# Another split of the tokens over the partitions, and counts and search one slot later, in attention followed by mixture of depths

## The chip, the cores and the metric

One core of a Trainium2 chip runs the whole kernel. The metric is the device time of one execution in microseconds; the time before is the median of three runs, 308.45 us (307.94 to 308.86).

## What is computed

Two steps, joined by a change of layout. With B = 8 batches, 8 heads, 576 tokens, head width 64, in float32:

```
q_s = softmax(q, over the 64 of a head)       k_s = softmax(k, over the 576 tokens)
attn = q_s @ (k_s.T @ v)                      per batch and head
x    = attn with its heads side by side       (8, 576, 512)

scores = x @ w_gate                           (8, 576)
top    = the 128 tokens of each batch with the highest score
out    = x
out[top] = x[top] + sigmoid(scores[top]) * (relu(x[top] @ w1) @ w2)
```

w1 is 512 x 1024, w2 is 1024 x 512. The input q, k and v are 9.4 MB each.

## The kernel before, in words

The work is cut into 16 units: unit u is batch u // 2 and four of its heads (`units`, L76). For a unit the 576 tokens lie five to a partition on partitions 0 to 63 (tokens 0 to 319) and four to a partition on partitions 64 to 127 (tokens 320 to 575), so a tile of q, k or v is 128 x 4 heads x 5 tokens x 64, and the fifth place of the upper half stays zero. `load(u, which)` (L84) brings each tensor with two DMAs on SyncE's queue (SP), one for each half: 64 partitions, 4 heads, pieces of 1,280 or 1,024 bytes. Three buffers each for q, k and v (`LD`) let loads run ahead; `load(u)` waits until the exponentials and the copy of unit u - 3 have read the buffer.

`prepare(u)` (L458) takes the exponentials of q and k on ScalarE and copies v next to a column of ones on VectorE. `kv_mm` (L178) multiplies k's exponentials with v, `kv_out` (L190) makes the block-diagonal right operand from it (with a last column for the gate's scores), `q_t` and `q_t_last` (L206, L218) transpose q's exponentials on TensorE, `x_mm` (L227) multiplies, and `x_out` (L239) normalizes on VectorE and, with a unit's second half done, stores x with two DMAs on SP. `score(b)` adds up a batch's gate scores.

The choice of the 128 tokens of batch b: `score_row(b)` (L267) spreads all scores over a row on every partition (transposes on TensorE, copies on ScalarE); `compare(b)` (L281) compares on VectorE each token's score with the row, tokens of equal score by their order; `count(b)` (L296) adds these up with matmuls against ones, which gives each token its rank; `pick(b)` (L314) searches, on VectorE, for the token of each rank (lines L322), makes its index, and POOL issues a gather of the 128 rows from the stored x (L327). Then `turn(b)` (L337) transposes the gathered rows on TensorE, `mlp1` and `mlp2` (L348, L363) are eight pieces each, 4 x 2 matmuls of 128 columns or 1 x 2 of 512, and `finish(b)` (L370) adds the result and scatters it from POOL.

The order on every engine is written out by hand (L473 to L551). Slot s does unit s, and kv_mm and q_t of unit s + 1, prepares unit s + 2 and loads unit s + 5; from slot 4 on, eight pieces of the MLP are spread over each slot, mlp1 of batch (s - 4) // 2 in even slots, mlp2 in odd ones. An odd slot ends with score_row; in the even slot that follows stand compare, later count and pick, and the even slot after that begins with turn. The parts of w1 and w2 are loaded on SP behind the loads of slots 0 to 4 (L528), so the first mlp1 pieces need the fourth part of w1, issued in slot 2. Each engine works in program order, and so does each DMA queue.

PSUM has three groups of banks, "tp" and "mm" with two banks each, "x" with two of double size. Before the first loads have come, 30 small matmuls keep TensorE busy (`WARM`, L107). A second path (`general`, with `shift`) runs only where sums leave a range, which they don't here; it changes with the layout and costs nothing.

Of the kernel before, what the change touches and what calls it, by code (L numbers as in the profile page):

```python
# [17 lines left out]
def kernel(  # L18
# [23 lines left out]
    P = 128  # L42
    R = 5
    N2 = R - 1
    S2 = 64 * R
# [7 lines left out]
    WARM = 30  # L53
    assert S == 64 * (R + N2) and D == 64 and DM == H * D and DM == 512 and H % 4 == 0
    assert 1 < capacity < S and KF == 8 and NQ == 2
    HALF = S // 2
# [39 lines left out]
    load(0, "qkv")  # L96
    load(1, "qkv")
    load(2, "qkv")
# [26 lines left out]
    nc.vector.memset(side, 0.0)  # L125
    v_ones, kv_diag = [], []
    for n in range(2):
        t = const.tile([P, 4, R, D + 1], F32, name=f"v_ones{n}")
        nc.vector.memset(t[:, :, :, D:], 1.0)
        nc.vector.memset(t[part(1), :, N2, D:], 0.0)  # L130
# [13 lines left out]
    tok_row = const.tile([P, S], F32, name="tok_row")  # L144
    rows4 = tok_row[:, :N2 * P].rearrange("p (r h c) -> p r h c", r=N2, h=2)
    nc.gpsimd.iota(rows4[:, :, 0], pattern=[[1, N2], [R, 64]], base=0, channel_multiplier=0,
                   allow_small_or_imprecise_dtypes=True)
    nc.gpsimd.iota(rows4[:, :, 1], pattern=[[1, N2], [N2, 64]], base=S2, channel_multiplier=0,
                   allow_small_or_imprecise_dtypes=True)
    nc.gpsimd.iota(tok_row[:, N2 * P:], pattern=[[R, 64]], base=N2, channel_multiplier=0,  # L150
                   allow_small_or_imprecise_dtypes=True)
# [87 lines left out]
    def x_out(u, i):  # L239
# [20 lines left out]
    chunks = [(slice(0, P), slice(r * P, (r + 1) * P)) for r in range(N2)] + [(slice(0, 64), slice(N2 * P, S))]  # L260

    def score(b):
        s = md.tile([P, R], F32, tag="s", name="s")
        nc.vector.reduce_sum(out=s, in_=sr.pop(b).rearrange("p a i r h -> p r (a i) h"), axis=AX.XY)
        st["s", b] = s

    def score_row(b):  # L267
        s = st["s", b]
        srow = md.tile([P, S], F32, tag="srow", name="srow")
        t_ps = bank("tp", 2)  # L270
        for r in range(N2):
            nc.tensor.transpose(out=t_ps[:, r * P:(r + 1) * P], in_=s[:, r:r + 1].to_broadcast([P, P]),
                                identity=ident)
        nc.scalar.copy(out=srow[:, :N2 * P], in_=t_ps)
        l_ps = bank("tp", 2)
        nc.tensor.transpose(out=l_ps[:, :64], in_=s[:64, N2:].to_broadcast([64, P]),
                            identity=ident[:64, :64])
        nc.scalar.copy(out=srow[:, N2 * P:], in_=l_ps[:, :64])
        st["srow", b] = srow

    def compare(b):  # L281
        s, srow = st["s", b], st["srow", b]
        less = md.tile([P, R, S], BF16, tag="less", name="less", bufs=1)
        ties = md.tile([P, R, P], BF16, tag="ties", name="ties", bufs=1)
        for j, (rows, cols) in enumerate(chunks):
            own = s[rows, j:j + 1]
            nc.vector.tensor_scalar(less[rows, j, :cols.stop], srow[rows, :cols.stop], own, None, op0=OP.is_lt)  # L287
            if cols.stop < S:
                nc.vector.tensor_scalar(less[rows, j, cols.stop:], srow[rows, cols.stop:], own, None,  # L289
                                        op0=OP.is_le)  # L290
            width = cols.stop - cols.start
            nc.vector.scalar_tensor_tensor(ties[rows, j, :width], srow[rows, cols], own, after[rows, :width],  # L292
                                           op0=OP.is_equal, op1=OP.mult)
        st["cmp", b] = less, ties

    def count(b):  # L296
        less, ties = st.pop(("cmp", b))
        rank = md.tile([P, S], F32, tag="rank", name="rank")
        for e in range(2):
# [3 lines left out]
            for j, (rows, cols) in enumerate(chunks):  # L303
                todo.append((rows, less[rows, j, lo:hi], 0, HALF))
                a, z = max(lo, cols.start), min(hi, cols.stop)
                if a < z:
                    todo.append((rows, ties[rows, j, a - cols.start:z - cols.start], a - lo, z - lo))
            for n, (rows, rhs, a, z) in enumerate(todo):
                nc.tensor.matmul(out=r_ps[:, a:z], lhsT=ones_b[rows, :P], rhs=rhs, start=(n == 0),  # L309
# [4 lines left out]
    def pick(b):  # L314
# [3 lines left out]
        for n, (k0, m) in enumerate(slots):  # L318
            sel = sl.tile([P, 2], F32, tag="sel", name="sel")
            for c, row in enumerate((tok_row, srow)):  # L320
                junk = md.tile([P, S], BF16, tag="junk_p", name="junk_p")
# [63 lines left out]
    def shift(u):  # L385
# [4 lines left out]
        nc.vector.tensor_max(m[part(0)], m[part(0)], kr[part(0), :, N2])  # L390
# [12 lines left out]
        for h in range(4):  # L403
            for n, rows in enumerate((R, N2)):
                o = kr[part(n), h, :rows]
                nc.vector.tensor_sub(o, o, row[part(n), h][:, None].to_broadcast([64, rows, D]))
# [5 lines left out]
    def general():  # L412
        for b in range(B):
            for u in (NQ * b, NQ * b + 1):
                load(u, "qkv")
# [42 lines left out]
    def prepare(u):  # L458
        q_exp(u)
        k_exp(u)  # L460
        v_copy(u)

# [10 lines left out]
    with tc.manual_schedule():  # L473
        prepare(0)
        load(3, "qkv")
# [8 lines left out]
        load(4, "qkv")  # L484

        number = None
        for s in range(NU + LAG):
# [14 lines left out]
            chosen = (s - 2) // 2 if s % 2 == 0 and 2 <= s <= NU else None  # L502
# [23 lines left out]
            if s + 5 < NU:  # L526
                load(s + 5, "qkv")
# [4 lines left out]
            if chosen is not None:  # L532
                compare(chosen)
# [5 lines left out]
            pieces(2)  # L539
            if ends is not None:  # L540
                score_row(ends)
# [3 lines left out]
            pieces(3)  # L545
            if last:
                pieces(1)
            if busy and odd == 1:
# [31 lines left out]
```

## Time and profile before

| | us |
|---|---|
| median of three runs | 308.45 (307.94 to 308.86) |
| the profiled execution's own time | 308.41 |
| its span in the profile | 306.6 |
| TensorE busy (matmuls) | 252.0, 82% |
| VectorE busy | 135.3, 44% |
| ScalarE busy | 98.7, 32% |
| POOL busy | 19.2, 6% |
| mean granted TensorE clock | 0.905 |

The span runs from the first instruction to the last; 1.8 us of the time lie outside it. A busy share is a mean over the whole span, and busy matmuls are not matmuls at full speed: the granted clock has two levels, 1.2 GHz (shown as 0.50) and 2.4 GHz (1.00). The chain of waits follows the end of the span backwards, from each instruction to what released it. The timeline lists an engine's instructions in order, equal ones merged (xN), with the idle time before them in brackets. Windows give each engine's busy time in a stretch, the granted clock, the share in which the 16 DMA engines were busy, and the bytes per second that they moved.

### The profile page before, as it was taken

The page shows a single profiled execution, that of the slowest core. Times are in us where ns is not written, and L with a number is a line of the kernel's source. Part 1 is how long each engine was busy: PE and PEld are TensorE (multiplying, and loading weights), DVE is VectorE, ACT ScalarE, POOL GpSimd, SP SyncE. Part 2 cuts the span into 40 slices and gives each one's busy share as a digit, 9 for nine tenths or more (in the row PEclk, how much of TensorE's full clock was granted, in tenths as well). Part 3 has the DMA queues.
Part 4 walks back from the last instruction along what each step waited for, and adds up shares of the span by engine and source line. Part 5 has one row for each costly group of instructions (what it writes and reads, how often), then busy time and mean ns, then how long its engine had stood idle before and what let it go on. Part 6 is the DMA issues. An engine that isn't in the chain of part 4 may idle for free.

```text
span 306.6 us, 5131 instructions
## 1 busy us (share of the span) xinstructions
PE 252.0 (82%) x1991; PEld 196.8 (64%) x1991; DVE 135.3 (44%) x494; ACT 98.7 (32%) x178; POOL 19.2 (6%) x33
## 2 busy tenths in 40 slices
PE   4267784825689998999989998999799989998991
PEld 4246682714677686867867685769585967583850
DVE  2125647711174538252754376336624484351000
ACT  2355542511042533252516251526134311120100
POOL 4000000100001010101010100010010101101101
PEclk9999977765599999699979997999689998999997
DMA  6999999999999596909792779331213031301000
GB/s 148 230 231 232 241 272 234 284 291 235 290 253 270 166 249 165 236 2 219 167 252 51 199 172 239 78 79 44 69 34 80 34 79 34 77 36 36 34 6 37
DMA packets 39328, 46.67 MB, mean 152 GB/s; under 512 B 2945, under 2 KB 36737, under 8 KB 39297
## 3 DMA queue, kind: packets, MB, share of 16 engines
q1 hardware_dynamic: 37472, 41.95, 57.9%
q0 software_dynamic: 1280, 4.20, 4.1%
q8 instruction: 17, 0.28, 0.4%
q10 hardware_dynamic: 544, 0.13, 0.2%
q14 instruction: 15, 0.11, 0.1%
HBM read 34.73 MB, written 11.53 MB: 151 GB/s over the span
## 4 chain that ended last, share of the span: by engine, by line
PE 67%; DVE 16%; DMA 9%; issue 2%; ACT 2%; SPq 1%; POOL 0%; POOLq 0%; DVEq 0%; ACTq 0%
PE mm L367 19%; PE mm L357 16%; PE x L233 12%; PE tp L186 8%; PE tp L213 6%; PE tp L309 4%; DVE less L287 4%; DMA out_dram<-xs 4%; DMA w<-in_moe_w_dram 3%; DVE ties L292 3%; DMA v<-in_v_dram 3%; DVE less L289 2%; DVE xs L249 2%; DVE v_ones L176 2%; SPq L91 1%
## 5 line engine op out<-in xcount | busy, mean ns | idle before, releaser
L357 PE MATMUL mm<-xT,w 128*128 128x128 f32 x512 | 73.5, 303 | 7.7 <-DMA w<-in_moe_w_dram 6.3
L357 PEld LDWEIGHTS mm<-xT,w 128*128 128x128 f32 x512 | 68.9, 216 | 10.5 <-DMA w<-in_moe_w_dram 6.6
L367 PE MATMUL mm<-w,hT 128*128 128x512 f32 x128 | 60.9, 602 | 0.0
L233 PE MATMUL x<-kv_diag,qT 128*128 128x132 f32 x320 | 43.7, 287 | 0.0
L233 PEld LDWEIGHTS x<-kv_diag,qT 128*128 128x128 f32 x320 | 41.7, 202 | 2.4 <-issue 2.4
L186 PE MATMUL tp<-v_ones,ke 128*64 128x65 f32 x640 | 26.8, 250 | 14.0 <-DVE after L158 8.8
L186 PEld LDWEIGHTS tp<-v_ones,ke 128*64 128x64 f32 x640 | 24.4, 162 | 17.1 <-issue 10.5
L367 PEld LDWEIGHTS mm<-w,hT 128*128 128x128 f32 x128 | 22.0, 190 | 17.5 <-issue 16.7
L215 ACT ACTIVATE qT<-tp,krec 128x512 f32<-128x512 f32 x32 | 22.0, 687 | 32.4 <-PE tp L213 32.3
L249 DVE TENSOR_TENSOR xs<-x,qrec 128x384 f32<-128x384 f32 x64 | 31.4, 491 | 2.2
L309 PE MATMUL tp<-less,ones_b 128*128 128x288 bf16 (+1 forms) x80 | 21.8, 329 | 12.2 <-DVE less L287 5.3
L309 PEld LDWEIGHTS <-ones_b 128*128 128x128 bf16 (+1 forms) x128 | 11.5, 104 | 27.0 <-issue 20.5
L248 DVE RECIPROCAL qrec<-x 128x6 f32<-128x6 f32 x64 | 11.8, 184 | 36.6 <-PE x L233 36.2
L375 DVE SCALAR_TENSOR_TENSOR o<-mm,g,xr 128x512 f32<-128x512 f32 x8 | 6.0, 751 | 44.3 <-PE mm L367 44.3
L172 ACT ACTIVATE qe<-q 128x640 f32<-128x640 f32 x32 | 21.6, 726 | 4.5 <-DMA q<-in_q_dram 4.5
L213 PE MATMUL tp<-ident,qe 128*128 128x128 f32 x128 | 22.7, 307 | 0.2 <-DVE prod L200 0.2
L165 ACT ACTIVATE ke<-k 128x1280 f32<-128x1280 f32 x16 | 20.1, 1258 | 1.2 <-DMA k<-in_k_dram 1.2
L360 ACT ACTIVATE hT<-mm 128x512 f32<-128x512 f32 x16 | 9.6, 598 | 31.5 <-PE mm L357 31.5
L213 PEld LDWEIGHTS tp<-ident,qe 128*128 128x128 f32 x128 | 17.2, 159 | 3.8 <-issue 2.6
L195 DVE RECIPROCAL krec<-tp 128x2 f32<-128x2 f32 x16 | 2.7, 170 | 38.0 <-PE tp L186 38.0
L327 POOL DMA_INDIRECT xr<-out_dram,idx x8 | 7.9, 987 | 177.2 <-DVE g L333 77.7
L311 ACT COPY rank<-tp 128x288 f32<-128x288 f32 x16 | 6.4, 399 | 36.2 <-PE tp L309 36.2
(65 smaller groups left out, 190.6 us busy)
## 6 DMA issues: line engine op xcount, KB each, us to landing
q<-in_q_dram SPq DMA_DIRECT2D x16, 320.0 KB, 10.1
k<-in_k_dram SPq DMA_DIRECT2D x16, 320.0 KB, 6.4
v<-in_v_dram SPq DMA_DIRECT2D x16, 320.0 KB, 6.8
out_dram<-xs SPq DMA_DIRECT2D x16, 320.0 KB, 4.0
q<-in_q_dram SPq DMA_DIRECT2D x16, 256.0 KB, 9.9
k<-in_k_dram SPq DMA_DIRECT2D x16, 256.0 KB, 6.3
v<-in_v_dram SPq DMA_DIRECT2D x16, 256.0 KB, 7.3
out_dram<-xs SPq DMA_DIRECT2D x16, 256.0 KB, 4.0
```

The lines of the kernel that those rows point to most:

```text
L165: nc.scalar.activation(out=ke, in_=raw["k"][u % LD], func=AF.Exp)
L172: nc.scalar.activation(out=qe[:, i], in_=qr[:, i], func=AF.Exp)
L186: nc.tensor.matmul(out=kv[part(h), i], lhsT=ke[:, 2 * i + h, r], rhs=vo[:, 2 * i + h, r], start=(r == 0), stop=(r == N2))
L213: nc.tensor.transpose(out=t_ps[:, r * P:(r + 1) * P], in_=qe[:, i, r].rearrange("p h d -> p (h d)"), identity=ident)
L215: nc.scalar.activation(out=st["qT", u][:, i, :N2].rearrange("p r c -> p (r c)"), in_=t_ps, func=AF.Copy, scale=krec[:, u, i:i + 1])
L233: nc.tensor.matmul(out=x[:, r // 3, r % 3], lhsT=qT[:, i, r], rhs=kv_diag[u % 2][:, i], start=True, stop=True)
L248: nc.vector.reciprocal(out=rec[:, rows], in_=o[:, :, :, D])
L249: nc.vector.tensor_mul(xs[b][:, rows, qd, i], o[:, :, :, :D], rec[:, rows].to_broadcast([P, rows.stop - rows.start, 2, D]))
L287: nc.vector.tensor_scalar(less[rows, j, :cols.stop], srow[rows, :cols.stop], own, None, op0=OP.is_lt)
L309: nc.tensor.matmul(out=r_ps[:, a:z], lhsT=ones_b[rows, :P], rhs=rhs, start=(n == 0), stop=(n == len(todo) - 1), skip_group_check=True)
L357: nc.tensor.matmul(out=h_ps[:, f % 4 * m:(f % 4 + 1) * m], lhsT=w1[:, d, f * P:(f + 1) * P], rhs=xT[:, d, :m], start=(d == 0), stop=(d == ...
L367: nc.tensor.matmul(out=st["y", b, n][:m], lhsT=st["hT", b, n][:, f, :m], rhs=w2[:, f], start=(f == 0), stop=(f == KF - 1))
```

## The change

The new tile has nine tokens in each pair of partitions: an even partition takes five, the odd one after it the next four. So each of the two DMAs of a tensor reaches every second partition of all 128, and so does each store. A row of scores has 640 places for 576, of which 64 are no tokens: `valid` is 1 on even and 0 on odd partitions, `beyond` is 0 and the lowest number, and the fifth score is valid * s + beyond. So the choice is made over five full chunks of 128 instead of four and a half.

The fifth places are zeroed over all partitions before the loads, on VectorE for the first buffers and on POOL for the others. Loads, and the exponentials of prepare, come in the order k, v, q. The warm-up is 20 float32 matmuls of 132 columns and 20 small ones.

In the order by hand, compare stays in the even slot; count and pick move to the odd slot behind it, after q_t_last and one more piece; score_row moves behind three more pieces. In the last slot of the units (15), score_row and compare of the last batch follow directly on the count of the batch before; slot 16 counts and picks the last batch. `turn` stays at the head of its even slot.

```
@@ def load @@
-            for n, (rows, s0) in enumerate(((R, 0), (N2, S2))):
+            for n, rows in enumerate((R, N2)):
                 nc.sync.dma_start(
-                    out=t[part(n), :, :rows].rearrange("p h r d -> p h (r d)"),
-                    in_=bass.AP(tensor=src.tensor, offset=first + s0 * D,
-                                ap=[[rows * D, 64], [SD, 4], [1, rows * D]]))
-
-    load(0, "qkv")
-    load(1, "qkv")
-    load(2, "qkv")
+                    out=t[n::2, :, :rows].rearrange("p h r d -> p h (r d)"),
+                    in_=bass.AP(tensor=src.tensor, offset=first + n * R * D,
+                                ap=[[9 * D, 64], [SD, 4], [1, rows * D]]))
+
+    for n in range(LD):
+        for what in "kvq":
+            (nc.vector if n == 0 else nc.gpsimd).memset(raw[what][n][:, :, N2], 0.0)
+    load(0, "kvq")
+    load(1, "kvq")
+    load(2, "kvq")
...
+    ones_f = const.tile([P, P + 4], F32, name="ones_f")
+    nc.vector.memset(ones_f, 1.0)
     w_ps = bank("tp", 2)
+    for n in range(20):
+        nc.tensor.matmul(out=w_ps[part(n % 2), :132], lhsT=ones_f[:, :64], rhs=ones_f, start=True, stop=True)
     for n in range(WARM):
         nc.tensor.matmul(out=w_ps[:, :P], lhsT=ones_b[:, :P], rhs=ones_b[:, :P], start=True, stop=True)
-    for n in range(LD):
-        for what, engine in (("q", nc.gpsimd), ("k", nc.vector), ("v", nc.gpsimd)):
-            engine.memset(raw[what][n][part(1), :, N2], 0.0)
...
@@ def x_out @@
-            for n, (rows, s0) in enumerate(((R, 0), (N2, S2))):
+            for n, rows in enumerate((R, N2)):
                 nc.sync.dma_start(
-                    out=bass.AP(tensor=out.tensor, offset=out[b, s0].offset + 4 * D * qd,
-                                ap=[[rows * DM, 64], [DM, rows], [1, 4 * D]]),
-                    in_=xs[b][part(n), :rows, qd].rearrange("p r i h d -> p r (i h d)"))
+                    out=bass.AP(tensor=out.tensor, offset=out[b, n * R].offset + 4 * D * qd,
+                                ap=[[9 * DM, 64], [DM, rows], [1, 4 * D]]),
+                    in_=xs[b][n::2, :rows, qd].rearrange("p r i h d -> p r (i h d)"))
@@ def score @@
+        nc.vector.scalar_tensor_tensor(s[:, N2:], s[:, N2:], valid, beyond, op0=OP.mult, op1=OP.add)
@@ def score_row @@
+        srow = md.tile([P, RP], F32, tag="srow", name="srow")
+        for r0, r1 in ((0, N2), (N2, R)):
+            t_ps = bank("tp", 2)
+            for r in range(r0, r1):
+                nc.tensor.transpose(out=t_ps[:, (r - r0) * P:(r - r0 + 1) * P],
+                                    in_=s[:, r:r + 1].to_broadcast([P, P]), identity=ident)
+            nc.scalar.copy(out=srow[:, r0 * P:r1 * P], in_=t_ps[:, :(r1 - r0) * P])
@@ def compare @@
+        less = md.tile([P, R, RP], BF16, tag="less", name="less", bufs=1)
+        for r in range(R):
+            own, end = s[:, r:r + 1], (r + 1) * P
+            nc.vector.tensor_scalar(less[:, r, :end], srow[:, :end], own, None, op0=OP.is_lt)
+            if end < RP:
+                nc.vector.tensor_scalar(less[:, r, end:], srow[:, end:], own, None, op0=OP.is_le)
+            nc.vector.scalar_tensor_tensor(ties[:, r], srow[:, r * P:end], own, after,
                                            op0=OP.is_equal, op1=OP.mult)
...
@@ def prepare @@
-        q_exp(u)
         k_exp(u)
         v_copy(u)
+        q_exp(u)
@@ slots @@
-            chosen = (s - 2) // 2 if s % 2 == 0 and 2 <= s <= NU else None
+            compared = (s - 2) // 2 if s % 2 == 0 and 2 <= s < NU else None
+            chosen = (s - 3) // 2 if s % 2 == 1 and 3 <= s < NU else None
+            if s == NU:
+                chosen = B - 1
...
-            if chosen is not None:
-                compare(chosen)
+            if compared is not None:
+                compare(compared)
             pieces(1)
             if s + 1 < NU:
                 q_t_last(s + 1)
             else:
                 pieces(1)
-            pieces(2)
-            if ends is not None:
-                score_row(ends)
+            pieces(1)
             if chosen is not None:
                 count(chosen)
                 pick(chosen)
-            pieces(3)
+            if last:
+                score_row(ends)
+                compare(ends)
+            pieces(2)
             if last:
                 pieces(1)
+            pieces(1)
+            if ends is not None and not last:
+                score_row(ends)
+            pieces(1)
             if busy and odd == 1:
                 each(finish, mlp_b)
```

count and pick work over 640 columns for 576, two halves of 320 for 288, with the same operations.

## Rows read from the trace of the kernel before

**Rows 1.** The chain of waits in order of time (start us, us, what)

```profile
12.66 0.83 DVE v_ones L176
...
69.70 9.85 DMA w<-in_moe_w_dram
...
79.60 0.79 PE mm L357 x2
...
250.07 1.00 PE tp L309 x8
...
271.37 1.82 PE tp L309 x16
```

**Rows 2.** The page, part 2: mean busy share of the DMA engines, 40 slices

```profile
DMA  6999999999999596909792779331213031301000
```

**Rows 3.** Windows of 3 us, first and last: clock, DMA share, GB/s

```profile
3.00:6.00 3.00, 1.85 (x18) 1.58 (x15) 0.45 (x4) 0.01 (x1) 0.95 (x5) 1.00 1.05 231
...
30.00:33.00 3.00, 2.16 (x48) 2.12 (x49) 1.19 (x3) 0.91 (x3) 0.00 (x0) 1.00 1.12 236
```

**Rows 4.** Windows of 1 us, the same columns

```profile
44.00:45.00 1.00, 1.00 (x11) 1.00 (x10) 0.93 (x5) 0.58 (x1) 0.00 (x0) 1.00 1.10 363
...
100.00:101.00 1.00, 1.00 (x11) 1.00 (x10) 0.20 (x1) 0.41 (x1) 0.00 (x0) 1.00 1.05 387
...
157.00:158.00 1.00, 1.00 (x7) 1.00 (x6) 1.00 (x3) 0.00 (x0) 0.00 (x0) 0.50 1.00 256
...
162.00:163.00 1.00, 1.00 (x6) 0.44 (x3) 0.17 (x1) 0.53 (x2) 0.00 (x0) 1.00 0.36 102
```

**Rows 5.** The page, part 6: DMA issues, with size and us to landing

```profile
out_dram<-xs SPq DMA_DIRECT2D x16, 256.0 KB, 4.0
```

**Rows 6.** Timeline of TensorE, slots 1, 8, 9: start us, us, instruction, [idle before]

```profile
30.84 1.39 PE L186 MATMUL tp<-v_ones,ke 128*64 128x65 f32 x40 [2.18 <-DVE v_ones L176]
...
149.77 1.95 PE L357 MATMUL mm<-xT,w 128*128 128x128 f32 x16
...
151.68 0.30 PE L309 MATMUL tp<-less,ones_b 128*128 128x288 bf16 x1
...
156.43 4.37 PE L357 MATMUL mm<-xT,w 128*128 128x128 f32 x24
...
160.72 1.39 PE L186 MATMUL tp<-v_ones,ke 128*64 128x65 f32 x40
...
163.44 1.29 PE L233 MATMUL x<-kv_diag,qT 128*128 128x132 f32 x10
...
167.85 0.38 PE L222 MATMUL tp<-ident,qe 128*128 128x128 f32 x2
...
170.51 2.84 PE L367 MATMUL mm<-w,hT 128*128 128x512 f32 x6
```

**Rows 7.** Groups by line and shape: the memsets of k's fifth places on VectorE

```profile
L111 DVE MEMSET k<- 64x256 f32 x3 | 0.8, 272 | 0.1
```

**Rows 8.** Timeline of VectorE: compare(0), its end, and the search of batch 6

```profile
47.67 0.28 DVE L287 TENSOR_SCALAR less<-srow,s 128x128 bf16<-128x128 f32 x1
...
51.58 0.41 DVE L224 TENSOR_TENSOR qT<-tp,krec 128x256 f32<-128x256 f32 x1
...
251.54 0.82 DVE L322 SCALAR_TENSOR_TENSOR junk_p<-rank,slot_no,tok_row 128x576 bf16<-128x576 f32 x1 [1.52 <-ACT rank L311]
```

**Rows 9.** Timeline of POOL: the gather of batch 6

```profile
253.95 0.97 POOL L327 DMA_INDIRECT xr<-out_dram,idx  x1 [14.50 <-DVE g L333]
```

**Rows 10.** us to landing: gathers issued at 253.95, 159.38, scatter at 174.43

```profile
DMA to landing us min/median/max: 3.4/3.4/3.4
...
DMA to landing us min/median/max: 3.9/3.9/3.9
...
DMA to landing us min/median/max: 7.4/7.4/7.4
```

**Rows 11.** Timeline of the SP queue: the first store of slot 9

```profile
168.63 0.57 SPq L254 DMA_DIRECT2D out_dram<-xs  x1
```

More of the change, by code (lines that the diff above doesn't have):

```diff
@@ L44 @@
     N2 = R - 1
-    S2 = 64 * R
+    RP = R * P
+    LOWEST = -3.4028235e38
     KD = DM // P
@@ L125 @@
     nc.vector.memset(side, 0.0)
+    p_int = const.tile([P, 1], I32, name="p_int")
+    nc.gpsimd.iota(p_int, pattern=[[0, 1]], base=1, channel_multiplier=1)
+    nc.vector.tensor_single_scalar(p_int, p_int, 1, op=OP.bitwise_and)
+    valid = const.tile([P, 1], F32, name="valid")
+    nc.vector.tensor_copy(out=valid, in_=p_int)
+    beyond = const.tile([P, 1], F32, name="beyond")
+    nc.vector.tensor_scalar(beyond, valid, 1.0, -LOWEST, op0=OP.subtract, op1=OP.mult)
     v_ones, kv_diag = [], []
@@ L128 @@
         t = const.tile([P, 4, R, D + 1], F32, name=f"v_ones{n}")
-        nc.vector.memset(t[:, :, :, D:], 1.0)
-        nc.vector.memset(t[part(1), :, N2, D:], 0.0)
+        nc.vector.memset(t[:, :, :N2, D:], 1.0)
+        nc.vector.tensor_copy(out=t[:, :, N2, D:], in_=valid[:, None].to_broadcast([P, 4, 1]))
         v_ones.append(t)
@@ L268, in score_row @@
         s = st["s", b]
[L269 to L278, printed above, removed]
+        srow = md.tile([P, RP], F32, tag="srow", name="srow")
[5 more added lines that the diff above has]
+            nc.scalar.copy(out=srow[:, r0 * P:r1 * P], in_=t_ps[:, :(r1 - r0) * P])
         st["srow", b] = srow
@@ L282, in compare @@
         s, srow = st["s", b], st["srow", b]
-        less = md.tile([P, R, S], BF16, tag="less", name="less", bufs=1)
+        less = md.tile([P, R, RP], BF16, tag="less", name="less", bufs=1)
         ties = md.tile([P, R, P], BF16, tag="ties", name="ties", bufs=1)
[L285 to L292, printed above, removed]
+        for r in range(R):
[4 more added lines that the diff above has]
+            nc.vector.scalar_tensor_tensor(ties[:, r], srow[:, r * P:end], own, after,
                                            op0=OP.is_equal, op1=OP.mult)
@@ L302, in count @@
             todo = []
-            for j, (rows, cols) in enumerate(chunks):
-                todo.append((rows, less[rows, j, lo:hi], 0, HALF))
-                a, z = max(lo, cols.start), min(hi, cols.stop)
+            for r in range(R):
+                todo.append((less[:, r, lo:hi], 0, HALF))
+                a, z = max(lo, r * P), min(hi, (r + 1) * P)
                 if a < z:
-                    todo.append((rows, ties[rows, j, a - cols.start:z - cols.start], a - lo, z - lo))
-            for n, (rows, rhs, a, z) in enumerate(todo):
-                nc.tensor.matmul(out=r_ps[:, a:z], lhsT=ones_b[rows, :P], rhs=rhs, start=(n == 0),
+                    todo.append((ties[:, r, a - r * P:z - r * P], a - lo, z - lo))
+            for n, (rhs, a, z) in enumerate(todo):
+                nc.tensor.matmul(out=r_ps[:, a:z], lhsT=ones_b[:, :P], rhs=rhs, start=(n == 0),
                                  stop=(n == len(todo) - 1), skip_group_check=True)
@@ L389, in shift @@
         nc.vector.reduce_max(out=m, in_=kr[:, :, :N2].rearrange("p h r d -> p h d r"), axis=AX.X)
-        nc.vector.tensor_max(m[part(0)], m[part(0)], kr[part(0), :, N2])
+        last = at.tile([P, 4, D], F32, tag="s_last", name="s_last", bufs=1)
+        nc.vector.tensor_scalar(last, kr[:, :, N2], valid, beyond, op0=OP.mult, op1=OP.add)
+        nc.vector.tensor_max(m, m, last)
         col = at.tile([P, 2], F32, tag="s_col", name="s_col", bufs=1)
@@ L403, in shift @@
         for h in range(4):
-            for n, rows in enumerate((R, N2)):
-                o = kr[part(n), h, :rows]
-                nc.vector.tensor_sub(o, o, row[part(n), h][:, None].to_broadcast([64, rows, D]))
+            nc.vector.tensor_sub(kr[:, h], kr[:, h], row[:, h][:, None].to_broadcast([P, R, D]))
+        nc.vector.tensor_scalar(kr[:, :, N2], kr[:, :, N2], valid, None, op0=OP.mult)
         t = qr.rearrange("p h r d -> p (h r) d")
@@ L414, in general @@
             for u in (NQ * b, NQ * b + 1):
-                load(u, "qkv")
+                load(u, "kvq")
                 shift(u)
@@ L474 @@
         prepare(0)
-        load(3, "qkv")
+        load(3, "kvq")
         late_constants()
@@ L483 @@
         load_w1(0)
-        load(4, "qkv")
+        load(4, "kvq")
         number = None
@@ L526 @@
             if s + 5 < NU:
-                load(s + 5, "qkv")
+                load(s + 5, "kvq")
             if s < 3:
```

20 lines of the change are left out of this document (7 added, 13 removed).

## The prediction

> **What bounds the kernel now.** The chain of waits, read in order of time, comes first: early on it ends in a transfer, the last rows of w1, issued at 69.70 and waited for by the matmul at 79.60 [rows 1]. The page's DMA line says why: after the first slice, every slice up to 100 us is full [rows 2]. So the span has two parts: up to 79.6 us the DMA queue is the limit, after it TensorE. The windows price the first part: from 3 to 33 us, where nothing but q, k, v and the small gate weights is loaded, ten windows of 3 us lie at 229 to 236 GB/s, 231 in the first, 236 in the last [rows 3]. Each of these loads fills 64 partitions. Two short windows show that the queue can do more: at 44 us, while stores from half the partitions are under way, with pieces of a kilobyte as in the loads and down to 256 KB each [rows 5], 363 GB/s; at 100 us, at the end of w2, which fills 128 partitions, 387 [rows 4].
>
> In the second part the TensorE timeline shows, in each even slot, the counts waiting on the compares: from the first count's matmul at 151.68 to the next slot's matmuls at 160.72 go 9.04 us, and the 24 matmuls behind the count take 4.37 of them [rows 6], since the granted clock stands at 0.50 there, its 1.2 GHz level [rows 4]. The 16 before the count took 1.91 us, from 149.77 to 151.68 [rows 6], so 24 unhindered take 2.85. The six even slots 4 to 14 show 7.5 to 10.3 us for this stretch, 9.1 in the mean; slot 8, shown here, stands for all.
>
> **The sum** is made against the profiled execution: span 306.6, its time 308.41, so 1.8 lie around the span. The median of the runs is 308.45, which is the same.
>
> **1. Loads, before 79.6 us.** Eight units of three tensors of 576 KB must come in ahead of w1's last part: 14.16 MB, at 231 GB/s 61.3 us. Number, bytes and pieces of the loads stay, but the 64 partitions of each are now every second one of 128. No row shows such a transfer. Lower end 231: still only 64 partitions are written at a time. (Slower than that nothing suggests: sizes and pieces are those of the row.) Upper end 375: the full-width row, rounded down. I take 300, about halfway, since sizes and pieces are those of the load rows and the spread that of the w2 row. Gain 61.3 x (1 - 231/300) = 14.1.
>
> The Trainium skill (SBUF — State Buffer, Door 1: The DMA port swizzle) says that partitions 0 to 63 reach 8 of 16 ports and gives 196 GB/s measured for them against 328 for all 128; by it the loads would run at 328, and this term be 18. The trace's 231 against 387 agrees in direction.
>
> **2. Ahead of the loads** stand memsets now. VectorE's three cost 0.27 each at half the partitions, 256 elements as now [rows 7]; SP's first load waits for the first of them, the others lie beside SP's issues: +0.5 with the semaphore, bounds 0.3 and 0.8 (all three). POOL's six replace six. That the first matmuls start earlier (k and v ahead of q, a longer warm-up) is worth nothing while the DMA queue ends this part, but it lowers the floor under it, the search and gather of batch 0. Before, compare(0) ran from 47.67 to the product at 51.58 [rows 8]. v, third of three tensors then, was copied at 12.66 [rows 1]; as the second it comes about 2.5 us earlier, so the compare ends near 49. Slot 3's matmuls (163.44 to 167.85 in slot 9, less a piece of 0.9 [rows 6]: 3.5), count 2.0, search to gather 3.1 (step 4) and a landing of 3.4 to 6.6 follow: 61 to 64. I take the lower, 61; so this part can give 18.6 at most. Steps 1 and 2: **-13.6**, the last w1 rows at 66.
>
> **3. The count leaves the even slots.** Of the 9.04 us, 2.85 stay. A count without waits took 1.82 us for 16 matmuls [rows 1]; at 640 columns for 576 it is 2.0, paid in the odd slot, and a full fifth transpose adds 0.1 there. Saved: 9.04 - 2.85 - 2.1 = 4.1, six times, **-24.5**. The compares grow by some 0.2 us, hidden: TensorE asks for them a slot later.
>
> **4. What takes its place.** Search and gather now follow the count in the odd slot, and the next slot begins with turn(b), which TensorE reaches in order. Before, the count that ended at 251.07 [rows 1] was searched from 251.54 [rows 8], and POOL issued the gather at 253.95 [rows 9]: 2.88 after it, with 640 columns 3.07. TensorE has four pieces of mlp2 and score_row between: 8 matmuls of 0.43 (six began at 170.51 and were through, but for the last one's tail, 2.6 later [rows 6]) and 0.64, together 4.1. Unloaded, the gather lands in 3.4 [rows 10]: a stall of 3.07 + 3.4 - 4.1 = 2.4. In slots 5, 7 and 9 it meets loads. The gather issued at 159.38 landed in 3.9 [rows 10], at 163.3, 0.9 after the DMA engines ran dry at about 162.4 (0.36 busy in that microsecond [rows 4]): it lands when the backlog is gone. In slot 9: last transposes at 167.85 [rows 6], a piece, count from 168.9 to 170.9, gather issued at 174.0, TensorE at the turn at 175.0. SP issued the stores from 168.63 [rows 11]; bytes move from about 170.1, 0.59 MB at 363 and 1.77 MB at 300 GB/s take 7.5, dry at 177.6, landed 178.5: a stall of 3.5. SP waits for nothing of the search. On POOL only the scatter of finish stands behind the gather, and no engine waits for that soon. On TensorE kv_mm, with nothing else to wait for, stands behind turn. Three loaded stalls 10.5, two unloaded 4.8. In the last, at the end of slot 15, compare(7) stands on VectorE (3.9 before [rows 8], now 4.2) between the search and finish(5), which frees the PSUM bank that mlp1 takes next: 7.7 us after the count, against 6.1 unhindered: 1.6. Together **+16.9**.
>
> **5. Clock.** A stall can take the granted clock down. Bounds for one: 0 (an idle stretch of 2.18 us was followed by 40 matmuls in 1.39, full speed) and 1.7 (what the 24 matmuls of slot 8 lost, about 4.4 - 2.85) [rows 6]. For stalls of 2.4 I take 0, nearest to the 2.18 row, for 3.5 half of it: **+2.6**. The added operations on valid and beyond are short ones in VectorE's idle time.
>
> Sum: -13.6 - 24.5 + 16.9 + 2.6 = -18.6. Span 288.0, time **290**.
>
> **Rivals.**
>
> Full rate, 375 GB/s. For it speaks the row of w2; against it, that a load still has 64 partitions and shorter pieces. The floor binds, -18.6; all stalls but the last are 2.4: 12.0 + 1.6 - 24.5 = -10.9, and no clock is lost. Span 277.1, time 279.
>
> The gather lands late although loads are faster, as a scatter under loads did, in 7.4 [rows 10]. Against it speaks the 3.9. Stall 3.07 + 7.4 - 4.1 = 6.4, three times, and 1.7 of clock each: 19.2 + 4.8 + 1.6 + 5.1 - 24.5 = +6.2; with -13.6, time 301.
>
> Slower: the stall at the turn takes the place of the wait removed, and nothing pays for it, as the loads stay at 231 (their short pieces being the limit, or 64 partitions however spread). Then steps 1 and 2 give +0.5; in slot 9 the engines run dry at 179.4, landing 180.3, stall 5.3: 15.9 + 4.8 + 1.6 + 5.1 of clock - 24.5 = +2.9. Span 310.0, time 312. For it: the load rate hardly moved in 30 us, and w2's pieces are longer. Against it: the stores' 363 with short pieces. It decides from about 240 GB/s down, where steps 1 and 2 give 1.8 and the stalls cost 2.0 more than the waits did.
>
> The Trainium skill (SBUF — State Buffer, The DMA setup-cost knee) gives 224 GB/s for a single transfer of 256 KiB and puts it down to its size; by it the loads, of 256 and 320 KB, would not get faster, and the slower rival's 312 holds. The trace's stores of 256 KB in the window with 363 GB/s speak against it.
>
> **Chances.** Forecast 0.48 (at 270 to 340 GB/s 284 to 299), full rate 0.20, late gather 0.10, loads unchanged 0.22. The first three are faster, less 0.02 of the late gather: 0.76. Of the unchanged case, whose clock and stalls may each be some microseconds off, 0.18 are slower and 0.04 the same; with the 0.02, same 0.06. The bound is 0.3%, about what a measurement of this kernel tells from no change. Range: from the full-rate case to the unchanged one, 279 to 312.
>
> **What would show it.** Right: windows of loads alone near 300 GB/s; the last w1 rows at about 66; no wait on VectorE before the counts; in its place TensorE waits for the gather at each turn, 2 to 4 us. Wrong: loads at 230 to 245; no wait at the turn, or more than 5 us; a granted clock of 0.50 behind every turn, up to 7.6 us more in all (six times 1.7, less 2.6).

## The result and the profile after

| | before | after |
|---|---|---|
| median of four runs, us | 308.19 | 299.54 (297.34 to 300.68) |
| the profiled execution's own time / span | 308.41 / 306.6 | 297.34 / 295.5 |
| mean granted TensorE clock | 0.905 | 0.920 |
| TensorE busy (matmuls) | 252.0 | 237.3 |

The changed kernel takes 0.9709 of the time (95% interval 0.965 to 0.9769): 8.7 us less, where the prediction had 18.4 less (290). The time lies in the range, 279 to 312, and the direction is right; less than half of the size came. The profiled execution is the quickest of the four (the others had a mean clock of 0.909), so the times below are about 2 us kinder to the change than the median. A run more than 1.5% above the fastest of its kernel is left out of the medians below: one of the four of experiment 1, two of the four of experiment 2, and some of the kernel before.

**The loads** got faster than forecast. Windows of 3 us, after (us, busy time of PE, PEld, DVE, ACT, POOL, then clock, DMA share, GB/s), against [rows 3]:

```profile
9.00:12.00 3.00, 2.02 (x44) 1.70 (x44) 0.75 (x3) 1.73 (x4) 0.00 (x0) 1.00 1.08 358
18.00:21.00 3.00, 2.52 (x23) 2.28 (x21) 2.74 (x11) 2.47 (x4) 0.00 (x0) 1.00 1.09 357
```

The five windows from 6 to 21 us, in which only loads are under way, show 356 to 359 GB/s, in place of 229 to 236. The page's part 2 of after (mean busy share of the DMA engines, and granted clock, 40 slices of 7.4 us), against [rows 2]:

```profile
PEclk9997796957999799998999599989999899999997
DMA  6999999880589218551649119220221122101101
```

The queue is no longer full up to 100 us; it is full up to some 52, nearly so up to 66, and empty in the next slice. So the first part doesn't end in a transfer of w1 any more. What it ends in, the TensorE timeline of after shows (start us, us, instruction, [idle before]), against [rows 1] and [rows 6]:

```profile
51.03 0.30 PE L312 MATMUL tp<-less,ones_b 128*128 128x320 bf16 x1
...
54.10 0.57 PE L312 MATMUL tp<-less,ones_b 128*128 128x320 bf16 x3 [2.09 <-DVE qT L232]
...
64.60 1.11 PE L346 MATMUL mm<-ident,xr 128*128 128x128 f32 x4 [8.68 <-DMA xr<-out_dram,idx]
65.64 2.44 PE L194 MATMUL tp<-v_ones,ke 128*64 128x65 f32 x40
68.01 2.08 PE L360 MATMUL mm<-xT,w 128*128 128x128 f32 x8
69.88 0.92 PE L221 MATMUL tp<-ident,qe 128*128 128x128 f32 x4
...
79.89 1.39 PE L194 MATMUL tp<-v_ones,ke 128*64 128x65 f32 x40
...
122.72 2.79 PE L370 MATMUL mm<-w,hT 128*128 128x512 f32 x6
...
131.11 0.66 PE L346 MATMUL mm<-ident,xr 128*128 128x128 f32 x4 [4.19 <-DMA xr<-out_dram,idx]
131.70 2.25 PE L194 MATMUL tp<-v_ones,ke 128*64 128x65 f32 x40
133.88 1.86 PE L360 MATMUL mm<-xT,w 128*128 128x128 f32 x8
...
164.22 1.11 PE L346 MATMUL mm<-ident,xr 128*128 128x128 f32 x4 [4.24 <-DMA xr<-out_dram,idx]
```

turn(0) waits 8.68 us for the gather of batch 0, and everything behind it runs at half speed: 40 matmuls of kv_mm take 2.44, in the next slot 1.39. The first transposes of q_t(5, 0) begin at 69.88. In before they begin at 80.19, right behind the w1 wait [rows 1], as its TensorE timeline shows:

```profile
80.19 1.06 PE L213 MATMUL tp<-ident,qe 128*128 128x128 f32 x4
```

So the change gives **-10.3** in the first part. From there to the end the kernel before takes 226.4 us, after 225.6: **-0.8** for all the rest, where the prediction had -24.5 + 16.9 + 2.6 = -5.0.

In the rest, the waits on VectorE ahead of the counts [rows 6] are gone, and TensorE waits at each turn instead. The waits by engine and line of after (us in total, times, longest):

```profile
PE mm L346 <- DMA xr<-out_dram,idx: 27.2, 7, 8.7
...
PE tp L312 <- ACT rank L314: 2.6, 5, 0.5
```

Seven stalls, 27.2 us; less the first, six of together 18.5. The second row is a wait that the prediction didn't have: inside the five counts of slots 5 to 13 the second half waits 0.51 for the PSUM bank that ScalarE empties. Slot by slot:

| slot of the turn | 4 | 6 | 8 | 10 | 12 | 14 | 16 |
|---|---|---|---|---|---|---|---|
| stall, us | 8.68 | 3.70 | 4.19 | 4.24 | 2.59 | 2.43 | 1.39 |
| kv_mm behind it (1.39 at full clock) | 2.44 | 2.24 | 2.25 | 2.44 | 2.44 | 2.36 | none |

The gathers that these stalls wait for, in the chain of waits of after (start us, us, what), against [rows 10]:

```profile
57.83 6.73 DMA xr<-out_dram,idx
...
93.23 5.03 DMA xr<-out_dram,idx
...
126.06 5.01 DMA xr<-out_dram,idx
...
193.03 3.43 DMA xr<-out_dram,idx
```

And the clock behind the turn of slot 8, a window of 1 us of after, against [rows 4]:

```profile
132.00:133.00 1.00, 1.00 (x26) 1.00 (x24) 0.00 (x0) 0.39 (x1) 0.87 (x1) 0.50 0.00 0
```

TensorE is busy for the whole microsecond, at the 1.2 GHz level.

So the change removed one wait and put another, with a slower clock behind it, in its place. Three questions for experiments: are the loads faster because of the partitions (and what is that worth alone); what does the move of count and search cost, in the first part and in the rest; and what does the clock take?

### The profile page after: what moved, and what is told of

Read it like the earlier page. It is cut to its first block, busy times and chain, and to the rows that moved or that the text cites. A ratio compares the mean times of both kernels' runs of the same rounds, so it can differ in the third digit from the quotient of the medians.

```text
span 295.5 us, 5206 instructions
## 1 busy us (share of the span) xinstructions
PE 237.3 (80%) x2021; PEld 191.7 (65%) x2021; DVE 143.9 (49%) x506; ACT 99.1 (34%) x178; POOL 22.1 (7%) x32
## 4 chain that ended last, share of the span: by engine, by line
PE 65%; DMA 18%; issue 7%; DVE 3%; POOL 2%; ACT 2%; SPq 1%; POOLq 0%; ACTq 0%
PE mm L360 20%; PE mm L370 15%; DMA xr<-out_dram,idx 11%; PE x L241 10%; PE tp L194 8%; PE tp L221 4%; PE tp L312 4%; DMA q<-in_q_dram 3%; PE mm L346 2%; DMA out_dram<-xs 2%; DMA k<-in_k_dram 2%; DVE junk_p L325 2%; POOL tok_row L158 1%; ACT rank L314 1%; PE tp L230 1%
## 5 line engine op out<-in xcount | busy, mean ns | idle before, releaser
L360 PE MATMUL mm<-xT,w 128*128 128x128 f32 x512 | 65.2, 284 | 1.4 <-ACT xT L348 1.4
L360 PEld LDWEIGHTS mm<-xT,w 128*128 128x128 f32 x512 | 61.8, 199 | 2.5 <-ACT xT L348 1.9
L194 PE MATMUL tp<-v_ones,ke 128*64 128x65 f32 x640 | 29.6, 265 | 8.0 <-DVE v_ones L184 4.3
L194 PEld LDWEIGHTS tp<-v_ones,ke 128*64 128x64 f32 x640 | 27.1, 177 | 11.3 <-ACT qe L180 4.8
L257 DVE TENSOR_TENSOR xs<-x,qrec 128x384 f32<-128x384 f32 x64 | 31.4, 491 | 2.2
L346 PE MATMUL mm<-ident,xr 128*128 128x128 f32 x32 | 7.2, 367 | 27.2 <-DMA xr<-out_dram,idx 27.2
L346 PEld LDWEIGHTS mm<-ident,xr 128*128 128x128 f32 x32 | 4.7, 180 | 32.9 <-DMA xr<-out_dram,idx 32.4
L221 PE MATMUL tp<-ident,qe 128*128 128x128 f32 x128 | 21.6, 296 | 4.5 <-DVE krec L203 3.1
L348 ACT COPY xT<-mm 128x512 f32<-128x512 f32 x8 | 4.7, 586 | 42.2 <-PE mm L346 42.2
```

The costliest lines, as they stand in the source:

```text
L194: nc.tensor.matmul(out=kv[part(h), i], lhsT=ke[:, 2 * i + h, r], rhs=vo[:, 2 * i + h, r], start=(r == 0), stop=(r == N2))
L221: nc.tensor.transpose(out=t_ps[:, r * P:(r + 1) * P], in_=qe[:, i, r].rearrange("p h d -> p (h d)"), identity=ident)
L257: nc.vector.tensor_mul(xs[b][:, rows, qd, i], o[:, :, :, :D], rec[:, rows].to_broadcast([P, rows.stop - rows.start, 2, D]))
L346: nc.tensor.transpose(out=t_ps[:, d * m:(d + 1) * m], in_=xr[:m, d * P:(d + 1) * P], identity=ident[:m, :m])
L360: nc.tensor.matmul(out=h_ps[:, f % 4 * m:(f % 4 + 1) * m], lhsT=w1[:, d, f * P:(f + 1) * P], rhs=xT[:, d, :m], start=(d == 0), stop=(d == ...
```

## Experiments

Each kernel ran four times; the kernel before, run beside them on the same chips, had a median of 307.37 (beside experiments 1, 2, 4 and 5), 306.82 (beside 3, 6 and 7) and 305.1 (beside 8). Ratios are to that kernel before, with a 95% interval in brackets. "After" is the changed kernel. In the edits, `...` stands for lines left out.

**1. The same pieces on neighbouring partitions.** All of the changed kernel stays, its slots too, but the five-token half lies on partitions 0 to 63, the four-token half on 64 to 127 (the token numbers and `valid` follow, not shown). Each load's pieces in DRAM are the same, byte for byte.

```diff
-                    out=t[n::2, :, :rows].rearrange("p h r d -> p h (r d)"),
+                    out=t[part(n), :, :rows].rearrange("p h r d -> p h (r d)"),
...
-                    in_=xs[b][n::2, :rows, qd].rearrange("p r i h d -> p r (i h d)"))
+                    in_=xs[b][part(n), :rows, qd].rearrange("p r i h d -> p r (i h d)"))
...
```

> The changed kernel with the nine tokens of a pair put on partitions i (five) and 64 + i (four) instead of 2i and 2i + 1: each load and store reads and writes the same pieces of DRAM as in the changed kernel, in 64 neighbouring partitions as before. All else stays. Theory A (the spread over partitions is what makes loads faster): loads alone back at 230 to 236 GB/s, the first MLP slot near 78, 308 to 313 us, no better than the kernel before. Theory B (the other order in DRAM or the order k, v, q makes them faster): 350 GB/s or more, 299 us.

Measured: 312.68, ratio 1.0263 (1.0135 to 1.039). Windows of 3 us of this kernel:

```profile
9.00:12.00 3.00, 1.03 (x19) 1.06 (x21) 0.96 (x2) 0.00 (x0) 0.00 (x0) 0.78 1.12 230
30.00:33.00 3.00, 2.26 (x41) 2.17 (x42) 1.04 (x3) 0.63 (x2) 0.00 (x0) 0.69 1.12 229
```

Its TensorE timeline:

```profile
71.07 1.12 PE L344 MATMUL mm<-ident,xr 128*128 128x128 f32 x4 [9.39 <-DMA xr<-out_dram,idx]
...
77.19 0.49 PE L358 MATMUL mm<-xT,w 128*128 128x128 f32 x2 [1.28 <-DMA w<-in_moe_w_dram]
77.51 0.60 PE L219 MATMUL tp<-ident,qe 128*128 128x128 f32 x4
...
145.21 1.12 PE L344 MATMUL mm<-ident,xr 128*128 128x128 f32 x4 [6.41 <-DMA xr<-out_dram,idx]
```

The rate is that of before: it hangs on which partitions one transfer reaches, not on its pieces. The w1 wait is back, and at slots 8 and 10 the stalls are 6.41 and 6.91 where after has 4.19 and 4.24. This is the prediction's slower rival: 312 forecast, 312.7 measured. That its total fits so well is partly luck: its first part was to be +0.5 and is -2.7 (q_t(5, 0) at 77.51, in before 80.19), its rest was to be +2.9 and is +6.8 (233.2 against 226.4). Without the new split the move, with the new start, makes the kernel slower, since the whole interval of the ratio lies above 1. The Trainium skill (SBUF — State Buffer, "Can I just issue two DMAs to hit both halves?") says that two concurrent transfers, one to each half, are hardly faster than one, and that only a single transfer that spans all 128 partitions uses all ports. The 230 here against 356 to 359 agrees, with the addition that every second partition is span enough.

**2. The new split with the slots of before.** count and pick go back into the even slot, behind the compares.

```diff
-            compared = (s - 2) // 2 if s % 2 == 0 and 2 <= s < NU else None
-            chosen = (s - 3) // 2 if s % 2 == 1 and 3 <= s < NU else None
+            chosen = (s - 2) // 2 if s % 2 == 0 and 2 <= s <= NU else None
...
-            pieces(1)
+            pieces(2)
+            if ends is not None:
+                score_row(ends)
             if chosen is not None:
...
```

> The changed kernel with the slots of before: count and search again in the even slot directly behind the compares, score_row ahead of them; the new split of the tokens, the order k, v, q and the warm-up stay. Theory A (the faster loads are worth about 20 us by themselves, and the move of count and search gave none of its 24.5 us): batch 0's gather is issued a slot earlier, the first MLP slot begins near 60, and from there the old 226 us follow with their waits on VectorE before the counts: about 288 us, faster than the changed kernel by 10. Theory B (the loads gave the 9 us measured, and the move is neutral): 299 us, the same as the changed kernel. Theory C (the move gave the gain): 308 us.

Measured: 281.24 (279.54 and 282.94), less than any of the three theories had. Its TensorE timeline:

```profile
54.72 1.12 PE L346 MATMUL mm<-ident,xr 128*128 128x128 f32 x4
...
58.87 0.60 PE L221 MATMUL tp<-ident,qe 128*128 128x128 f32 x4
...
131.43 0.30 PE L312 MATMUL tp<-less,ones_b 128*128 128x320 bf16 x1 [0.62 <-DVE less L292]
...
133.04 4.33 PE L360 MATMUL mm<-xT,w 128*128 128x128 f32 x24
```

turn(0) waits for nothing and starts at 54.72, against 64.60 in after; q_t(5, 0) at 58.87 is 21.3 earlier than in before. The count's waits and the half-speed mlp1 behind them (4.33 for 24 matmuls) are as in [rows 6]. So the split and the new start alone give 26 us (307.37 to 281.24), and **the move, as it was placed, takes more than half of them back**: 14.4 between the profiled spans (281.1 and 295.5), 18.3 between the medians (281.24 and 299.54).

**3. Only batch 0's count and search back in slot 2.** It tells the first part's share of that loss from the rest's.

```diff
+            if s in (2, 3):
+                chosen = 0 if s == 2 else None
```

> The changed kernel, with count and search of batch 0 alone put back into slot 2, directly behind its compare; all other batches as in the changed kernel. Theory A (the first part ends with batch 0's gather, which the move made 9 us later): turn(0) near 55 without a wait, the rest unchanged, 289 to 292 us. Theory B (the first part is held by w1 or by the loads): turn(0) or the first mlp1 piece still waits to about 64, 298 to 300 us.

Measured: 288.05, ratio 0.9397 (0.9319 to 0.9475). Its TensorE timeline:

```profile
54.77 0.66 PE L346 MATMUL mm<-ident,xr 128*128 128x128 f32 x4 [0.23 <-DMA xr<-out_dram,idx]
...
57.66 0.60 PE L221 MATMUL tp<-ident,qe 128*128 128x128 f32 x4
...
86.74 1.11 PE L346 MATMUL mm<-ident,xr 128*128 128x128 f32 x4 [4.66 <-DMA xr<-out_dram,idx]
```

One batch out of eight is most of the loss: 10.3 between the profiled spans (285.2 and 295.5), 11.5 between the medians. turn(0) is 9.8 earlier, and without the long wait the way from it to q_t(5, 0) takes 2.9 us (54.77 to 57.66) instead of 5.3; the other stalls stay (4.66, 3.72, 3.91, 2.52, 2.52, 1.47). At the end of slot 3, where the change puts batch 0's count, only score_row follows it and there is no MLP work yet, so nothing covers the way from the count to the gather's landing, and the whole kernel stands behind it.

**4. Dummy matmuls in the stalls.** Ahead of the turns of slots 6 to 16 TensorE runs matmuls whose result nobody reads, as many as fit into the stall. The waiting stays; only the idleness goes.

```diff
+            if first and 6 <= s <= NU:
+                f_ps = bank("tp", 2)
+                for _ in range({6: 17, 8: 17, 10: 17, 12: 10, 14: 10, 16: 5}[s]):
+                    nc.tensor.matmul(out=f_ps, lhsT=ones_b[:, :P], rhs=ones_b, start=True, stop=True)
```

> The changed kernel with matmuls that compute nothing (bf16, 512 columns, 0.21 us each at full clock) in front of turn in slots 6 to 16: 17 in slots 6, 8 and 10, 10 in slots 12 and 14, 5 in slot 16, about as long as the stall there. The waits for the gather stay. Theory A (idle TensorE at turn loses the clock, some 1.7 us each): the matmuls behind turn run at 1.00 again, 288 to 292 us, 8 to 11 faster than the changed kernel. Theory B (the low clock behind turn comes from something else, the bf16 counts for instance): no gain, 299 us or slightly more.

Measured: 288.04, ratio 0.937 (0.9277 to 0.9463). The turn of slot 8 in its TensorE timeline:

```profile
125.76 3.83 PE L514 MATMUL tp<-ones_b 128*128 128x512 bf16 x16
129.43 0.66 PE L346 MATMUL mm<-ident,xr 128*128 128x128 f32 x4
130.02 1.39 PE L194 MATMUL tp<-v_ones,ke 128*64 128x65 f32 x40
131.33 1.16 PE L360 MATMUL mm<-xT,w 128*128 128x128 f32 x8
```

kv_mm behind the turn is back at 1.39, mlp1's first piece at 1.16 instead of 1.86. turn(0) starts at 64.56 as in after, and from there to the end it takes 222.6 us, in after 230.9: the clock alone costs 8.3 in the profiled executions, 11.5 between the medians. Idling costs twice: the stall, and about half as much again behind it.

**5. Count and search half a slot earlier.** In the odd slot, ahead of the second x_mm. So 7.1 us of TensorE's work lie between the count's end and the turn (130.06 to 137.16 below), where after has 4.2 (122.72 to 131.11, less the stall of 4.19); search and unloaded gather need 3.1 + 3.4. Slot 16 stays as it is.

```diff
+            if chosen is not None and s < NU:
+                count(chosen)
+                pick(chosen)
             if s < NU:
                 x_mm(s, 1)
...
-            if chosen is not None:
+            if chosen is not None and s >= NU:
```

> The changed kernel with count and search of odd slots moved ahead of the second half of x (after the second piece of the MLP), compare still in the even slot before. Now some 7 us of TensorE's work lie between the count and turn. Theory A (the stalls at turn cost 18.5 us and the low clock behind them some 10): no wait at turn above 0.5 us in slots 6 to 14, granted clock 1.00 there, 270 to 275 us. Theory B (the gather would be late anyway, or the search now delays x_out and with it the next slot): waits of a few us move to x_out, kv_mm or score_row, 290 us or more.

Measured: **257.61** (257.23 to 259.03), ratio 0.8414 (0.8336 to 0.8492), the fastest kernel up to here and better than forecast. Its TensorE timeline:

```profile
55.71 1.12 PE L346 MATMUL mm<-ident,xr 128*128 128x128 f32 x4 [0.20 <-DMA xr<-out_dram,idx]
...
60.71 0.60 PE L221 MATMUL tp<-ident,qe 128*128 128x128 f32 x4
...
110.75 0.60 PE L346 MATMUL mm<-ident,xr 128*128 128x128 f32 x4
111.28 1.39 PE L194 MATMUL tp<-v_ones,ke 128*64 128x65 f32 x40
...
128.42 0.30 PE L312 MATMUL tp<-less,ones_b 128*128 128x320 bf16 x1
...
130.06 1.34 PE L241 MATMUL x<-kv_diag,qT 128*128 128x132 f32 x10
...
137.16 0.60 PE L346 MATMUL mm<-ident,xr 128*128 128x128 f32 x4
```

No turn behind the first waits; the count, whose compares are long done, takes 1.64 (128.42 to 130.06) with no wait in it; a pair of slots takes 26.4 us (110.75 to 137.16), in after 31.3 to 33.7. From q_t(5, 0), at 60.71, to the end it takes 194.9, against 226.4 in before. The expectation was 12 us too high at its lower end. It took from the 299.5 of after only the stalls and the clock behind them, and left out two things that the trace shows: the first part is shorter, with q_t(5, 0) at 60.71 instead of 69.88 (9.2), and the five waits inside the counts are gone (2.6). Batch 0's count still stands in slot 3, but ahead of the second x_mm: its gather is issued at 51.80 instead of 57.83 and lands in 3.9 instead of 6.73.

**6. The same early count in the kernel before.** Old split, old start, new slots.

```diff
-            chosen = (s - 2) // 2 if s % 2 == 0 and 2 <= s <= NU else None
+            compared = (s - 2) // 2 if s % 2 == 0 and 2 <= s < NU else None
+            chosen = (s - 3) // 2 if s % 2 == 1 and 3 <= s < NU else None
...
+            if chosen is not None and s < NU:
+                count(chosen)
+                pick(chosen)
             if s < NU:
                 x_mm(s, 1)
...
```

> The kernel before, with its layout, loads and start, and only count and search moved: in the odd slot ahead of the second half of x, as in the early count. Theory A (the two changes add up: the slow loads hold the first MLP slot near 80, and from there the 195 us of the early count follow): 275 to 279 us. Theory B (with slow loads the gather or the loads themselves come late in every pair of slots): 285 us or more, waits for the gather at turn or for loads in slots 6 to 12.

Measured: 284.0, ratio 0.9236 (0.9162 to 0.9311), between the two expectations: nearer to Theory B's time, but without the waits from slot 6 on that Theory B had. Its TensorE timeline:

```profile
68.50 1.11 PE L343 MATMUL mm<-ident,xr 128*128 128x128 f32 x4 [5.40 <-DMA xr<-out_dram,idx]
78.54 0.80 PE L357 MATMUL mm<-xT,w 128*128 128x128 f32 x2 [5.55 <-DMA w<-in_moe_w_dram]
...
103.07 4.47 PE L367 MATMUL mm<-w,hT 128*128 128x512 f32 x6 [2.24 <-DMA w<-in_moe_w_dram]
```

The first part ends in the wait for w1 as in before, and w2 is waited for too; from slot 6 on the pairs take 27.0 each without a wait, where those of before take 31.4 to 32.7. The four pairs of before lie between these turns of its TensorE timeline:

```profile
109.21 0.60 PE L343 MATMUL mm<-ident,xr 128*128 128x128 f32 x4
...
237.25 0.60 PE L343 MATMUL mm<-ident,xr 128*128 128x128 f32 x4
```

So the split with the new start is worth 26 us alone (experiment 2), the move, if placed as in experiment 5, 23 (306.82 to 284.0), and both together 50.

**7. The old start under the early count.** Loads and exponentials in the order q, k, v again, the old warm-up of 30 small matmuls.

```diff
-    load(0, "kvq")
+    load(0, "qkv")
...
-    for n in range(20):
-        nc.tensor.matmul(out=w_ps[part(n % 2), :132], lhsT=ones_f[:, :64], rhs=ones_f, start=True, stop=True)
...
```

> The early count of the run before (257.6 us), with the order q, k, v of loads and exponentials and the warm-up of before (30 small matmuls). Theory A (k and v first and the longer warm-up bring the first matmuls some 3 us forward, and with fast loads nothing else holds the first part): 259 to 262 us. Theory B (the start is hidden behind the transfers, as the prediction had it): 257 to 258 us.

Measured: 263.37, a little more than Theory A had, ratio 0.8559 (0.8495 to 0.8624), against 0.8414 with the new start. Its TensorE timeline:

```profile
10.97 2.44 PE L190 MATMUL tp<-v_ones,ke 128*64 128x65 f32 x40 [5.31 <-DVE after L162]
...
61.45 1.06 PE L342 MATMUL mm<-ident,xr 128*128 128x128 f32 x4
```

With the new start the first kv_mm takes 1.39, at 9.34, and turn(0) stands at 55.71. The new start is worth 5.8 us between the medians, about 4.5 by the ratios, once the loads don't end the first part. The prediction had it at nothing while the DMA queue ends this part, and that condition is gone. This edit doesn't separate the order of the loads from the warm-up.

**8. Dummies in the first part too.** Experiment 5 with matmuls that nobody reads in the idle stretches of slots 2 and 3, to keep the clock up before turn(0).

```diff
...
+                if s == 3:
+                    fill(12)
                 q_t(s + 1, 0)
...
                 q_t_last(s + 1)
+                if s in (2, 3):
+                    fill(9 if s == 2 else 15)
```

> The early count (257.6 us) with matmuls that compute nothing in the first part: 9 behind the last transposes of slot 2, 12 in slot 3 ahead of q_t(4, 0), 15 behind the last transposes of slot 3, each about as long as TensorE's idle stretch there, 0.21 us apiece at full clock. Theory A (idle stretches of 2 to 3 us cost the granted clock for the matmuls behind them, in the first part as at turn): the matmuls of x in slot 3, turn(0), kv_mm(5) and the first mlp1 piece run at 1.00, 254 to 255.5 us. Theory B (the first part ends with a transfer all the same): no gain, 257 to 258 us.

Measured: 256.25, ratio 0.8402 (0.8321 to 0.8484) against 0.8414 (0.8336 to 0.8492): no difference that can be told. Its TensorE timeline:

```profile
45.03 1.29 PE L241 MATMUL x<-kv_diag,qT 128*128 128x132 f32 x10
...
55.90 0.91 PE L346 MATMUL mm<-ident,xr 128*128 128x128 f32 x4 [1.07 <-DMA xr<-out_dram,idx]
```

x_mm of slot 3 runs at full clock (1.29; in experiment 5 it took 2.41), yet turn(0) starts no earlier: it waits 1.07 for the gather, and kv_mm behind it takes 2.44 all the same. The gather was issued at 51.26, in experiment 5 at 51.80: the first part now ends in batch 0's search and gather, and a faster TensorE changes little.

## Why the prediction was right and wrong

All but one of the mechanisms were there. Two steps failed, both by the cost of what stands behind the turn, and the wait inside the counts was missing.

- **Step 1, the rate: right in kind, too small.** 300 was taken between 231 and 375; the windows of loads alone show 356 to 359. Since the loads no longer end the first part, the rate above 300 didn't size the gain. The fact that the prediction counted as unknown, whether 64 spread partitions load faster than 64 neighbouring ones, is shown by experiment 1.
- **Step 2, the floor: failed.** The prediction put the gather of batch 0 between 61 and 64, took 61, and set against it the w1 matmul at 79.60, so that the first part "can give 18.6 at most". The sum up to the gather's issue, 54.5 for the count's end plus 3.1, or 57.6, met the measured 57.83 by luck. compare(0) ended at 44.85 on VectorE and not near 49, but TensorE then took 6.2 us and not 3.5 to the count (at 51.03), and the count 3.9 and not 2.0, since its second half waits 2.09 for a PSUM bank.

  What failed is the rest. The gather landed after 6.73, not 3.4 (the bound was 6.6). And the floor is a landing, while the matmul at 79.60 is the last before q_t(5, 0): between a landing and q_t(5, 0) lie turn, kv_mm and the first mlp1 piece, 5.3 us in the half clock that the long wait leaves behind (64.60 to 69.88). In the prediction's terms: 3.6 for the later landing and 4.7 for those 5.3, less the 0.6 from 79.60 to 80.19, leave 10.3 of 18.6, the measured 80.19 - 69.88. Without the wait the 5.3 are 2.9 (experiment 3). The prediction's -13.6, from the rate, seemed to lie above this floor; the true floor bound. Experiment 3 shows that the move of batch 0's count put it there: 10.3 to 11.5 us. It is the place at the end of slot 3 that costs, not the slot: in experiment 5 the count stands half a slot earlier in slot 3, and turn(0) starts at 55.71.
- **Step 3, the waits removed: right, too small.** 4.1 per pair was forecast. In the kernel before, the early count (experiment 6) takes the pairs from 32.0 (109.21 to 237.25 are four) to 27.0, so 5.0; with the new split they are 26.4. Of that 0.6, 0.26 is the count (1.64 against 1.90). The 0.9 between 4.1 and 5.0 is in the traces too: the way from the first count matmul to the next slot's kv_mm, 9.04 in slot 8, is 9.65 in the mean of slots 6 to 12 (0.6), the 24 matmuls behind the count take 2.64 unhindered and not 2.85 (0.2; in experiment 6, 40 take 4.56, and the first 16 in before 1.92), and without the fifth transpose the odd slot pays 2.0 and not 2.1. Over all the rest experiment 5 gives 226.4 - 194.9 = 31.5, against 24.5.
- **Step 4, the stalls: right.** 16.9 forecast, 18.5 measured, three long ones (3.7 to 4.2 for 3.5), two of 2.4 to 2.6 (2.4), a last of 1.4 (1.6). Of the last only the size fits: it was summed as mlp1's wait for a PSUM bank, and is turn's wait for the gather.
- **Step 5, the clock: failed.** "For stalls of 2.4 I take 0, nearest to the 2.18 row, for 3.5 half of it: +2.6." Every stall with a kv_mm behind it, the 2.43 too, was followed by one of 2.24 to 2.44. Experiment 4 prices it at 8.3 to 11.5 us. The bound of 1.7 per stall was sound (five times 1.7 is 8.5, within what was measured), although the difference given for it, 4.4 - 2.85, is 1.55; with the 2.64 of step 3 it is 1.7; the choice inside the bounds was wrong. The prediction named this outcome, "a granted clock of 0.50 behind every turn", among what would prove it wrong.

The sum of the rest with measured terms: -31.5 for the waits, +2.6 for the new wait inside the counts, +18.5 for the stalls, +8.3 for the clock gives -2.1, where the trace has -0.8. That the rest came within 4.2 of the forecast is luck: step 3 gave 7.0 more than was forecast, and hid most of what the stalls (1.6), the missing wait (2.6) and the clock (5.7) cost beyond it. With the first part's -10.3 that is -12.4, and the profiled spans differ by 11.1.

The rival of the late gather gave 301, near the 299.5 measured, but not by its mechanism: it had the loads at 300 GB/s, landings of 7.4 and a first part of -13.6; the loaded landings in the rest were 5.0 to 5.1, and the time was lost at batch 0 and to the clock. Of the rival of the full rate, the rate nearly came true (356 to 359 for 375) and the time didn't, since its sum carried the same floor and "no clock is lost".

## What to carry to other kernels

When a step is moved into a later slot, ask of each turn of the loop, the first above all, what work stands between its result and the engine that needs it; here 7.1 us of work in that place instead of 4.2, and batch 0's gather issued 6.0 us earlier, turned 8.7 us of gain into 50. A floor must be compared with the same instruction in the kernel before, including all that follows in order behind the landing. And where a wait of some microseconds appears on TensorE, price the slow matmuls that may stand behind it along with it: here about half of the stalls again.

## What was not expected of the hardware

- 64 partitions, every second of 128, load at 356 to 359 GB/s, the same pieces onto 64 neighbouring ones at about 230 (experiment 1). Whole-width transfers of w2 in before reached 387 [rows 4].
- The clock's answer to an idle stretch isn't the same each time, and the length alone doesn't decide. In after, two waits of 2.17 us stand ahead of kv_mm; behind the first its 40 matmuls take 2.44, behind the second 1.39, full speed:

```profile
22.70 2.44 PE L194 MATMUL tp<-v_ones,ke 128*64 128x65 f32 x40 [2.17 <-DVE v_ones L184]
...
40.94 1.39 PE L194 MATMUL tp<-v_ones,ke 128*64 128x65 f32 x40 [2.17 <-DVE v_ones L184]
```

  What else decides, no run here shows; so the prediction's single row of 2.18 us [rows 6] couldn't settle its step 5.
- The count over 640 columns, whose long matmuls have 128 rows and 320 columns, takes 1.64 us (experiment 5), that over 576 columns, some of it with 64 rows, 1.90 (experiment 6, same place in the slot): the padding costs TensorE less than nothing here. Why the smaller count is slower was not tested.
